# Loading w_q in ten transfers instead of two: eight of 16 rows and two of 64 rows

## The chip, the core and the metric

The kernel runs on one core of a Trainium2 chip, as one launch. The metric is the device time of the launch in microseconds, median of three runs. A profiled execution of the same kernel gives the trace; its span runs from the first to the last instruction, and the device time is a little longer than the span.

## The reference, cut to what matters

One decode step (one new token, batch 2) of a block that normalises x, runs attention over the last 4096 entries of a key and value cache with 32 query heads on 8 key heads, and multiplies the result by a gate from a small gated MLP:

```
xn = layernorm(x)                          # x: 2 x 1 x 512
q  = (xn @ wq) as 32 heads of 128          # wq: 512 x 4096
k, v = the last 4096 rows of each of 2 x 8 cache heads, 128 wide
o  = softmax(q k^T / sqrt(128)) v          # 4 query heads share a cache head
s  = o @ wo                                # wo: 4096 x 512
z  = gelu(xn @ w_in)                       # w_in: 512 x 1792
g  = w_sp * layernorm(z[896:]) + b_sp
y  = (z[:896] * g) @ w_out                 # w_out: 896 x 512
out = x + s * silu(y)
```

All of it is float32. What has to be read is 8 MB of w_q, 3.5 MB of w_in, 1.75 MB of w_out, 64 MB of keys and values, and 8 MB of w_o.

## The kernel before, in words

All large data goes through one ring of four SBUF slots (`ring`, `bufs=4`), each 128 partitions x 8192 float32, so 32 KB a partition and 4 MB in all. The tiles in the order in which they take a slot are wq0, wq1 (the two halves of w_q), win, wout, then k0, k1, v0, k2, v1, ... for eight units of attention (a unit is two cache heads), and last the pieces of w_o. All of these loads are issued on the SP queue, in the order of the code; a load that reuses a slot waits until the engines have finished with what was there.

w_q is viewed as 128 partitions x 4 rows x 4096 (`wq_v`, L93): partition p holds rows 4p to 4p+3 of w_q, 64 KB in a piece in memory. The first half, wq0, is the first two of these four rows (32 KB in a piece), the second half, wq1, the other two. The loop at L95 to L98 loads each half with one transfer of 128 rows of 32 KB.

After the loads the code makes small constants on POOL and DVE, normalises x and turns it (xnT). Then PE forms q: the loop over k at L202 runs 32 matmuls on wq0 (k = 0, 1) and 32 on wq1 (k = 2, 3) into the PSUM banks q_ps. The first needs all of wq0, the 33rd all of wq1. Then comes the MLP (z from win, y from wout), then the eight attention units: DVE turns a key tile in four parts (kt), PE makes the scores (sh, s), ACT the exponentials (p), and PE weighs the values (acc). The last part multiplies by w_o, whose last pieces are small (8, 8, 8, 4, 2, 1 and 1 of its 32 row blocks), and writes the 4 KB result.

Three tiny loads are issued on ACT's queue at the start: xs (x itself, 4 KB) and the two scalars of wb1 (4 bytes each).

How a load reports that it has landed matters to the change. The program gives each load one of eight completion counters in turn (DMAHW0 to DMAHW7 in the listings below). A load that takes a counter again first waits, on the queue that issues it, until the load that had the counter before has landed.

Of the kernel before, what the change touches and what calls it, by code (L numbers as in the profile page):

```python
# [14 lines left out]
P = 128  # L15
# [27 lines left out]
def kernel(  # L43
# [14 lines left out]
    pe, dve, act, sp = (InOrder(tc, e) for e in (nc.tensor, nc.vector, nc.scalar, nc.sync))  # L58
# [22 lines left out]
    def slot(name):  # L81
        return ring.tile([P, SLOT], F32, tag="slot", name=name)
# [10 lines left out]
    wq_v = wq.rearrange("(p k) f -> p k f", p=P)  # L93
    wqt = []
    for a in range(2):  # L95
        t = slot(f"wq{a}")
        sp.dma_start(t, wq_v[:, 2 * a : 2 * a + 2, :].rearrange("p k f -> p (k f)"))
        wqt.append(t.rearrange("p (k f) -> p k f", k=2))  # L98
    win = slot("win")[:, : KT * F]
    sp.dma_start(win, w_in.rearrange("(p k) f -> p (k f)", p=P))  # L100
# [325 lines left out]
    for i, piece in enumerate(pieces):  # L426
        t = slot(f"wo{i}").rearrange("p (j d) -> p j d", d=D)
# [54 lines left out]
    for n in range(EARLY):  # L482
        t, a = blocks[n]
# [5 lines left out]
    for n in range(EARLY, 32):  # L489
        if n == LATE:  # L490
            spread_quarters(so, parts, start=False, stop=False)
        t, a = blocks[n]
# [37 lines left out]
```

## Time and profile before

| | |
|---|---|
| device time, median of 3 runs | 217.5 us (217.49 to 217.58) |
| profiled execution: device time | 217.5 us |
| profiled execution: span | 215.7 us, so 1.8 us lie outside it |
| busy: PE, DVE, ACT | 155.7, 108.5, 44.1 us |
| load queue of SP (q1) | 89.40 MB in 3912 packets, 96.8% of 16 engines' span |
| mean rate | 415 GB/s |

The page divides the span into 40 slices of 5.4 us and gives, for each, the busy share of every engine in tenths, the share for which the 16 DMA engines were busy, and the GB/s that they moved. The tables by stretch give the same for freely chosen stretches, with a DMA share that can come out a little over or under 1, since a packet is counted in the stretch in which it starts. A packet of q1 is one row of a tile, or a small message of a few bytes that reports that an engine has finished its part of a transfer.

### The profile page before, as it was taken

What the parts mean: (1) busy time and instruction counts of PE and PEld (TensorE: products, weight loads), DVE (VectorE), ACT (ScalarE), POOL (GpSimd) and SP (SyncE); (2) the same over time, 40 slices, a digit from 0 to 9 for tenths busy, and PEclk for the clock granted to TensorE, in tenths of its full rate; (3) what the DMA queues carried; (4) which work ended last, traced back from release to release, by engine and by line L of the source; (5) the groups of instructions that cost most, each with busy time, mean ns of one, the idle gap of its engine ahead of it and who ended that gap; (6) DMA issues with size and microseconds to landing.
All of it is one profiled execution on the core that took longest, in us unless ns stands there. A gap on an engine that the chain in (4) does not pass through costs nothing.

```text
span 215.7 us, 2229 instructions
## 1 busy us (share of the span) xinstructions
PE 155.7 (72%) x866; PEld 43.6 (20%) x866; DVE 108.5 (50%) x176; ACT 44.1 (20%) x109; POOL 2.6 (1%) x14
## 2 busy tenths in 40 slices
PE   0164856151796997899699599459959948998883
PEld 0110212110121222222122222222212212231311
DVE  3400072425976944963946851685577089240101
ACT  5000001401123115114303404120431421242001
POOL 4000000000000000000000000000000000000000
PEclk9999788755589699799889879958988995999699
DMA  7998999999999999999999999999999999999990
GB/s 292 389 486 389 425 433 454 451 416 431 444 395 474 395 459 413 450 425 431 437 400 456 413 444 428 431 437 431 431 407 453 419 444 431 431 401 416 425 377 35
DMA packets 3929, 89.54 MB, mean 415 GB/s; under 512 B 446, under 2 KB 462, under 8 KB 848
## 3 DMA queue, kind: packets, MB, share of 16 engines
q1 hardware_dynamic: 3912, 89.40, 96.8%
q8 instruction: 7, 0.11, 0.2%
q14 instruction: 2, 0.02, 0.0%
q10 hardware_dynamic: 8, 0.00, 0.0%
HBM read 89.40 MB, written 0.00 MB: 414 GB/s over the span
## 4 chain that ended last, share of the span: by engine, by line
DMA 44%; PE 31%; DVE 19%; issue 3%; ACT 1%; SPq 0%; DVEq 0%
DMA k<-in_A_k_cache_dram 22%; DMA win<-in_B_w_in_dram 14%; DVE kt L37 13%; PE s L37 9%; PE sh L37 9%; DMA wo<-in_A_wo_dram 8%; PE acc L37 6%; PE z L37 2%; PE y L37 2%; PE mo L37 1%; DVE gate L37 1%; PE col L37 1%; PE so L37 1%; DVE u L37 1%; DVE m L37 1%
## 5 line engine op out<-in xcount | busy, mean ns | idle before, releaser
L37 DVE STREAM_TRANSPOSE kt<-k 128x2048 f32<-128x2048 f32 x32 | 72.4, 2293 | 24.9 <-DMA k<-in_A_k_cache_dram 24.9
L37 PE MATMUL sh<-kt,qbd 128*32 128x512 f32 x256 | 41.5, 682 | 14.0 <-DVE kt L37 14.0
L37 PE MATMUL s<-shs,add_dq 128*128 128x512 f32 x64 | 41.0, 748 | 0.0
L37 ACT ACTIVATE shs<-sh 128x512 f32<-128x512 f32 x32 | 19.1, 597 | 100.9 <-PE sh L37 100.9
L37 PE MATMUL acc<-v,pT 128*32 128x512 f32 x256 | 32.0, 641 | 0.2 <-DVE pT L37 0.2
L37 PE MATMUL q_ps<-wq,xnT 128*32 128x512 f32 x64 | 11.0, 850 | 9.9 <-DMA wq<-in_A_wq_dram 9.9
L37 PEld LDWEIGHTS s<-shs,add_dq 128*128 128x128 f32 x64 | 11.2, 219 | 28.3 <-issue 23.9
L37 PEld LDWEIGHTS sh<-kt,qbd 128*32 128x32 f32 x256 | 6.9, 115 | 33.9 <-issue 19.6
L37 PEld LDWEIGHTS acc<-v,pT 128*32 128x32 f32 x256 | 7.7, 118 | 25.8 <-issue 23.0
L37 DVE TENSOR_REDUCE m<-s 128x2 f32<-128x512 f32 x8 | 5.4, 680 | 14.0 <-PE s L37 14.0
L37 PE MATMUL mo<-l,same_r 128*128 128x2 f32 x16 | 3.5, 287 | 10.7 <-ACT p L37 10.7
L37 DVE STREAM_TRANSPOSE qT<-q_ps 128x512 f32<-128x512 f32 x2 | 1.4, 717 | 18.1 <-PE q_ps L37 18.1
L37 ACT ACTIVATE o<-acc,wd 128x128 f32<-128x128 f32 x32 | 9.1, 373 | 3.4 <-PE acc L37 3.4
L37 ACT ACTIVATE p<-s,nb 128x256 f32<-128x256 f32 x16 | 7.6, 490 | 7.1 <-DVE nb L37 6.9
L37 PE MATMUL part<-wo,oT 128*32 128x512 f32 x56 | 8.2, 722 | 1.1 <-DMA wo<-in_A_wo_dram 0.8
L37 PE MATMUL col<-o,sel 128*32 128x512 f32 x16 | 8.3, 601 | 0.4 <-ACT o L37 0.4
L37 ACT ACTIVATE zs<-z 128x448 f32<-128x448 f32 x1 | 0.5, 544 | 30.9 <-PE z L37 30.9
L37 PE MATMUL y<-wout,hT 128*32 128x512 f32 x14 | 3.6, 1059 | 3.8 <-issue 3.8
L37 PEld LDWEIGHTS q_ps<-wq,xnT 128*32 128x32 f32 x64 | 2.6, 144 | 17.1 <-issue 12.2
L37 DVE STREAM_TRANSPOSE pT<-p 128x512 f32<-128x512 f32 x8 | 5.4, 675 | 1.2 <-ACT p L37 1.2
L37 DVE TENSOR_TENSOR res<-so,gate 128x128 f32<-128x128 f32 x1 | 0.3, 292 | 11.1 <-PE so L37 11.1
L37 ACT ACT_TABLE_LOAD x4 | 5.1, 1283 | 1.9 <-issue 1.9
(106 smaller groups left out, 66.8 us busy)
## 6 DMA issues: line engine op xcount, KB each, us to landing
k<-in_A_k_cache_dram SPq DMA_DIRECT2D x8, 4096.0 KB, 21.3
v<-in_A_v_cache_dram SPq DMA_DIRECT2D x8, 4096.0 KB, 26.7
wq<-in_A_wq_dram SPq DMA_DIRECT2D x2, 4096.0 KB, 21.3
wo<-in_A_wo_dram SPq DMA_DIRECT2D x3, 2048.0 KB
win<-in_B_w_in_dram SPq DMA_DIRECT2D x1, 3584.0 KB, 29.3
wout<-in_B_w_out_dram SPq DMA_DIRECT2D x1, 1792.0 KB, 33.1
wo<-in_A_wo_dram SPq DMA_DIRECT2D x1, 1024.0 KB
wo<-in_A_wo_dram SPq DMA_DIRECT2D x1, 512.0 KB, 17.4
```

Of the source, the lines that this page charges most:

```text
L37: return self.tc.keep_in_program_order(call(*args, **kwargs))
```

## The change: what it does

The loop that loads the two halves of w_q issues several transfers for each half. The first half goes in eight transfers of 16 rows: transfer r takes partitions r, r+8, r+16, ..., r+120. The second half goes in two transfers of 64 rows: the even partitions, then the odd ones. Every row is still 32 KB in a piece, lands at the same place, and is loaded once.

```diff
     for a in range(2):
         t = slot(f"wq{a}")
-        sp.dma_start(t, wq_v[:, 2 * a : 2 * a + 2, :].rearrange("p k f -> p (k f)"))
+        rows = 16 if a == 0 else 64
+        for r in range(P // rows):
+            sp.dma_start(
+                t[r : P : P // rows, :],
+                wq_v[r : P : P // rows, 2 * a : 2 * a + 2, :].rearrange("p k f -> p (k f)"),
+            )
         wqt.append(t.rearrange("p (k f) -> p k f", k=2))
```

On the SP queue, at the start of the program, there stood before (wq_69 is the tile of the first half, wq_71 that of the second; in brackets what a load waits for, where `PE` and `DVE` mean the last reader of the slot):

```order
L37 DMA wq_69<-in_A_wq_dram 128x8192
L37 DMA wq_71<-in_A_wq_dram 128x8192
L37 DMA win<-in_B_w_in_dram 128x7168
L37 DMA wout<-in_B_w_out_dram 128x3584
L37 DMA k_281<-in_A_k_cache_dram 128x1x8192 [waits DMAHW1_49,PE_49]
L37 DMA k_283<-in_A_k_cache_dram 128x1x8192 [waits DMAHW4_49,DMAHW0_49,PE_49]
```

and now (wq_69 and wq_78 are the two halves):

```order
L37 DMA wq_69<-in_A_wq_dram 16x8192 x5
L37 DMA wq_69<-in_A_wq_dram 16x8192 [waits DMAHW0_49]
L37 DMA wq_69<-in_A_wq_dram 16x8192 [waits DMAHW1_49]
L37 DMA wq_69<-in_A_wq_dram 16x8192 [waits DMAHW2_49]
L37 DMA wq_78<-in_A_wq_dram 64x8192 [waits DMAHW3_49]
L37 DMA wq_78<-in_A_wq_dram 64x8192 [waits DMAHW4_49]
L37 DMA win<-in_B_w_in_dram 128x7168 [waits DMAHW5_49]
L37 DMA wout<-in_B_w_out_dram 128x3584 [waits DMAHW6_49]
L37 DMA k_289<-in_A_k_cache_dram 128x1x8192 [waits DMAHW2_49,DMAHW1_49,DMAHW7_49,DMAHW0_49,PE_49]
L37 DMA k_291<-in_A_k_cache_dram 128x1x8192 [waits DMAHW4_49,DMAHW3_49,PE_49]
```

Eight loads are added, and the first four loads of before, which waited for nothing, now stand behind waits on counters that are used a second time: DMAHW0 had xs, DMAHW1 the first piece of w_q, DMAHW2 and DMAHW3 the two scalars of wb1, DMAHW4 to DMAHW7 the second to fifth piece.

On PE, at the start of the q matmuls, there stood before:

```order
L37 MATMUL q_ps_149<-wq_69,xnT 32x512 [waits DMAHW1_49,DVE_49]
L37 MATMUL q_ps_149<-wq_69,xnT 32x512 x3
L37 MATMUL q_ps_150<-wq_69,xnT 32x512 x4
L37 MATMUL q_ps_149<-wq_69,xnT 32x512 x4
L37 MATMUL q_ps_150<-wq_69,xnT 32x512 x4
L37 MATMUL q_ps_149<-wq_71,xnT 32x512 [waits DMAHW4_49]
```

and now:

```order
L37 MATMUL q_ps_157<-wq_69,xnT 32x512 [waits DMAHW4_49,DMAHW5_49,DMAHW2_49,DMAHW6_49,DMAHW1_49,DMAHW7_49,DMAHW0_49,DVE_49]
L37 MATMUL q_ps_157<-wq_69,xnT 32x512 x3
L37 MATMUL q_ps_158<-wq_69,xnT 32x512 x4
L37 MATMUL q_ps_157<-wq_69,xnT 32x512 x4
L37 MATMUL q_ps_158<-wq_69,xnT 32x512 x4
L37 MATMUL q_ps_157<-wq_78,xnT 32x512 [waits DMAHW4_49,DMAHW3_49]
```

The matmuls and their order are the same; the first waits for all eight pieces of the first half, the 33rd for both of the second.

## The prediction, made before the changed kernel was run

> **What bounds the kernel now.** I read the page's slices and queues first, then a table by stretch, then single microseconds of the load queue, then the queue of SP and the end of the chain.
>
> The page, slices and queue (busy tenths of the 16 DMA engines, GB/s; packets, MB, share):
>
> ```profile
> DMA  7998999999999999999999999999999999999990
> GB/s 292 389 486 389 425 433 454 451 416 431 444 395 474 395 459 413 450 425 431 437 400 456 413 444 428 431 437 431 431 407 453 419 444 431 431 401 416 425 377 35
> ...
> q1 hardware_dynamic: 3912, 89.40, 96.8%
> ```
>
> By stretch (last two columns: DMA share and GB/s):
>
> ```profile
> 0.00:2.00 2.00, 0.00 (x0) 0.00 (x0) 0.57 (x2) 0.14 (x1) 1.45 (x11) 1.00 0.51 150
> 2.00:4.00 2.00, 0.00 (x0) 0.00 (x0) 0.99 (x3) 1.91 (x3) 1.18 (x4) 1.00 0.93 377
> 4.00:12.00 8.00, 0.61 (x4) 0.55 (x4) 3.05 (x20) 0.92 (x2) 0.00 (x0) 1.00 0.91 393
> 12.00:20.00 8.00, 5.67 (x32) 1.39 (x32) 0.00 (x0) 0.00 (x0) 0.00 (x0) 1.00 1.06 459
> 20.00:30.00 10.00, 5.34 (x32) 1.22 (x32) 2.77 (x10) 0.00 (x0) 0.00 (x0) 0.83 0.97 419
> ...
> 60.00:110.00 50.00, 42.60 (x218) 11.46 (x220) 35.08 (x40) 12.31 (x32) 0.00 (x0) 0.88 1.01 432
> 110.00:160.00 50.00, 40.47 (x220) 12.02 (x212) 29.05 (x36) 12.75 (x35) 0.00 (x0) 0.90 1.00 431
> 160.00:200.00 40.00, 34.29 (x182) 8.83 (x182) 20.25 (x30) 9.57 (x27) 0.00 (x0) 0.87 0.99 425
> ```
>
> The loads bound the kernel. From 2 us to the end of the last load the 16 engines are never idle, and they move 432 GB/s in a long stretch, 27.0 GB/s each; 89.40 MB at 432 GB/s is 206.9 us of a 215.7 us span. PE, DVE and ACT have room in every stretch. The chain of waits names other work too, but its last link of that kind is a load:
>
> ```profile
> 193.29 17.36 DMA wo<-in_A_wo_dram
> ...
> 210.70 1.24 PE so L37 x32
> ...
> 212.79 0.29 DVE res L37
> ```
>
> SP does wait for engines to free slots, yet it issues early enough that the share stays at 0.97 to 1.06. So a microsecond that the load engines lose at the start has nothing to be absorbed in, and moves the last w_o piece (210.66 us) and the end by a microsecond. PE work on w_q is no cover: it waits for the loads.
>
> One round of rows, from 7 to 8 us:
>
> ```profile
> DMA packets 17, 0.52 MB, mean 524 GB/s; under 512 B 1, under 2 KB 1, under 8 KB 1
> ...
> q1 hardware_dynamic: 16, 0.52, 121.3%
> q10 hardware_dynamic: 1, 0.00, 0.1%
> ```
>
> Sixteen rows of 32 KB start together: the engines go in step, one row each. 0.524 MB at 432 GB/s is 1.214 us a round, and a half of w_q is eight rounds, 9.71 us.
>
> **The change, part by part.**
>
> SP and its waits:
>
> ```profile
> 0.73 0.86 SPq L37 DMA_DIRECT2D wq<-in_A_wq_dram  x2
> 1.63 0.46 SPq L37 DMA_DIRECT2D win<-in_B_w_in_dram  x1
> 2.14 0.53 SPq L37 DMA_DIRECT2D wout<-in_B_w_out_dram  x1
> 18.63 9.83 SPq L37 DMA_DIRECT2D k<-in_A_k_cache_dram  x2
> ...
> 12.90 5.67 PE L37 MATMUL q_ps<-wq,xnT 128*32 128x512 f32 x32 [5.93 <-DMA wq<-in_A_wq_dram]
> 22.51 5.34 PE L37 MATMUL q_ps<-wq,xnT 128*32 128x512 f32 x32 [3.94 <-DMA wq<-in_A_wq_dram]
> ```
>
> *Issuing.* Eight more loads at 0.43 us (two took 0.86) are 3.4 us of SP. A piece feeds the engines for a 1.21 us round, so issuing stays ahead of moving: nothing. What is queued behind on SP is win and wout, then k0, which waits for PE until 18.63 us anyway.
>
> *Counters.* The sixth to eighth piece and wq1's first transfer wait for xs, the first piece and the two wb1 scalars; wq1's second, win and wout wait for pieces two to four, which land earlier. The scalars come last. Their queue is q10, eight packets in all; from 9 to 10 us, and from 10 to 12 us:
>
> ```profile
> q1 hardware_dynamic: 15, 0.49, 113.7%
> q10 hardware_dynamic: 1, 0.00, 0.1%
> ...
> q1 hardware_dynamic: 17, 0.56, 64.4%
> ```
>
> The last q10 packet starts before 10 us. Then wq1 can be issued, while the eight pieces keep the engines fed to about 12 us (4.20 MB have started by then by the first three stretches, one half of w_q). From first issue to the flow was 0.9 to 1.5 us (0.73 to about 2.28, where 4.20 MB at 432 GB/s would have begun). So the margin is 12.0 - 10.0 - 1.5 = 0.5 us at the least: nothing. If rounds take twice as long, so do the q10 packets, one to a round, and so does the supply; the margin grows. If that cover fails, see the rivals.
>
> *Reports of completion.* Eight more transfers put eight more small packets on each engine. q1 is busy 0.968 x 215.7 = 208.8 us and its bytes need 206.9; if all of the 1.9 us were the reports of 27 transfers, that is 0.07 us each and 0.56 us for eight. The other end is 0, since the 7-to-8 us row shows a small packet beside 16 full rows. I take 0.1, nearer to that row.
>
> *Where the rows land.* This decides. Before, a round of 16 rows can be dealt from all 128 partitions. Now each round of the first half is one transfer: 16 rows, at partitions r, r+8, ..., r+120, with seven of eight partitions untouched, for r = 0 to 3 one set of groups of four and for r = 4 to 7 the other. The steady 27.0 GB/s an engine, alike for weights and caches and for rows of 32 and 16 KB, looks like a fixed cap. If it is the engine's own, the stride costs 0. If it is a cap of paths into the tile, each serving some partitions, two engines share a path and a round takes 2 x 1.214 us: eight rounds cost 9.71 us more. No transfer in this trace with large rows leaves partitions out, so no row lies near either end; a gain is excluded from a rate that is already at the cap in all stretches. I take the shared path: a limit at memory would hardly be equal for such different sources, and half the groups of partitions idle in each round is the pattern in which a limit by partition must show. Two engines that aren't quite in step share a path a little less; for this I take off 0.3 us (0 to 1.2, one round).
>
> [...]
>
> *The second half.* Rows at stride 2 touch every group of four partitions. Each transfer has four rows for an engine, all groups in use: I take 0; the other end is 9.71, if engines in step aim at the same groups at the same time. The nearest row is that of 60 to 110 us: the cache loads have 64 x 2 rows as their source, and ran at 432.
>
> Sum: 217.5 (the profiled execution, equal to the median) + 9.7 - 0.3 + 0.1 = 227.0 us. Landings: wq0 12.9 to 22.4, wq1 22.5 to 32, win 31 to 40.5, all later ones 9.5 later. What is late next is nothing new: k0's issue waits for PE on wq0 (18.6 to 28), and wq1, win and wout keep the engines fed past 45 us.
>
> **The rivals.**
>
> *Engines don't share (no change).* Only reports remain: 217.5 + 0.1 = 217.6, from 217.3 to 218.1. For it: 27.0 GB/s may be the engine's own. Against: the argument above. 22%.
>
> *Both halves share.* 217.5 + 9.4 + 9.7 + 0.1 = 236.7. For it: engines in step. Against: the cache loads. 15%.
>
> *The counters starve the queue.* It decides from the point where the second wb1 scalar lands later than about 11 us. If ACT's packets only get through when SP's eight pieces are done (12 us), wq1 comes 0.9 to 1.5 us after, so 219.0 without sharing. Against: one q10 packet starts in each microsecond from 7 to 10. 6%.
>
> *The pieces don't go one row to an engine.* If partitions fix the engine, pieces 0 to 3 use eight engines with two rows each and 4 to 7 the others, which begin four issues (1.7 us) later: 219.3. The trace can't tell, all transfers having 128 rows. 5%. [...]
>
> *Faster.* A first transfer of one row each might start all engines sooner. 4.20 MB by 12.0 us leave 2.28 - 0.73 = 1.55 us from issue to flow; half of that saved gives 216.8. The only cover-free gain I see; nothing shows the start to depend on the size of the transfer. 4%.
>
> **How the numbers follow.** Sharing in the first half alone has 45%, with 226.0 to 228.0 as its own range; some sharing of smaller size (218 to 226) 3%. Taking in the cases from no change to the first half gives 217.2 to 228.0, with 15% (both halves) and 4% (faster) outside. 0.2% is 0.4 us, about what a measurement of this kernel can tell. Faster 5%: that rival, and a little of the case without sharing. Same 18%: most of the 22%. Slower 77%: the rest.
>
> **What would show it.** First PE matmul on wq0 at about 22.4 us, on wq1 at 32; in the stretch from 4 to 20 us some 216 GB/s, and 432 again from 24 us on. If wq0 lands at 13 us, the stride costs nothing and the forecast is wrong at its main step. If 216 GB/s lasts to 40 us, both halves share. If the DMA share drops below 0.9 with rows of the old length, it is the counters.

## The result, and the profile after

The changed kernel took 228.1 us (median of five runs, 228.0 to 228.75) against 217.54 us before: 10.6 us longer, a ratio of 1.0491, 95% interval 1.0476 to 1.0506. Forecast were 227.0 us and a range of 217.2 to 228.0; the way was right, the time lies 0.1 us above the range.

The page of the changed kernel, slices of 5.66 us and load queue:

```profile
DMA  8999899999999999999999999999999999999991
GB/s 186 185 220 237 376 440 405 446 423 459 408 423 457 411 428 454 411 428 452 417 428 439 423 434 440 420 434 434 417 440 440 414 440 434 423 411 428 420 390 42
...
q1 hardware_dynamic: 4040, 89.40, 96.9%
```

The load engines are as busy as before, but the first four slices move about half as much: 185 to 237 GB/s. The bytes are the same, and the 128 packets more are the reports of eight transfers on 16 engines. The table by stretch (last columns: DMA share and GB/s) shows where it ends:

```profile
0.00:2.00 2.00, 0.00 (x0) 0.00 (x0) 0.57 (x2) 0.03 (x1) 1.45 (x11) 1.00 0.01 2
2.00:22.50 20.50, 0.61 (x4) 0.55 (x4) 4.05 (x24) 2.94 (x4) 1.19 (x4) 1.00 1.03 221
...
24.00:34.00 10.00, 6.42 (x36) 1.57 (x37) 0.00 (x0) 0.00 (x0) 0.00 (x0) 0.89 1.00 429
34.00:200.00 166.00, 129.27 (x658) 35.15 (x654) 99.96 (x139) 37.14 (x92) 0.00 (x0) 0.82 1.00 431
```

From 24 us on the rate is 429 to 431 GB/s, that of the kernel before. So the second half, in two transfers of 64 rows at stride 2, loads at full rate; nearly all that is lost is lost on the first half. One round of it, from 6.6 to 9.15 us:

```profile
DMA packets 32, 0.52 MB, mean 206 GB/s; under 512 B 16, under 2 KB 16, under 8 KB 16
...
q1 hardware_dynamic: 32, 0.52, 100.6%
```

Sixteen rows and their sixteen reports in 2.55 us, where a round of before took 1.21. Sixteen rows keep the sixteen engines busy for that time (share 100.6%): one row to an engine, and each engine needs 2.1 times as long for it.

The trace has the start and the duration of every packet, and the rows of w_q give the whole loss round by round. The rows of the first round start 0.26 us later on average than in the kernel before, and take 0.58 us longer (2.25 for 1.67). Those of six rounds take 1.33 us longer (2.55 for 1.21), those of the fifth round, the first with r = 4 to 7, 1.18 us (2.39 for 1.21), and those of the first round of the second half 0.51 us (1.72 for 1.21). Together that is 10.5 us; from the next round on, the rows are 10.6 us later than before.

SP and PE in the changed kernel:

```profile
0.73 8.27 SPq L37 DMA_DIRECT2D wq<-in_A_wq_dram  x10
...
23.86 5.83 PE L37 MATMUL q_ps<-wq,xnT 128*32 128x512 f32 x32 [16.84 <-DMA wq<-in_A_wq_dram]
33.27 6.24 PE L37 MATMUL q_ps<-wq,xnT 128*32 128x512 f32 x32 [3.58 <-DMA wq<-in_A_wq_dram]
42.69 4.53 PE L37 MATMUL z<-win,xnT 128*32 128x448 f32 x32
```

PE starts on the first half at 23.86 us instead of 12.90, on the second at 33.27 instead of 22.51, 11.0 and 10.8 later. At the end, the chain's last link is a load as before, and PE begins its last work 10.7 us later than in the kernel before (210.70 there):

```profile
204.30 17.09 DMA wo<-in_A_wo_dram
221.38 0.04 issue
221.43 1.68 PE so L37 x40
```

Nothing absorbed the loss and nothing added to it on the way.

### The profile page after: what moved, and what is told of

Read it like the earlier page. It is cut to its first block, busy times and chain, and to the rows that moved or that the text cites. A ratio compares the mean times of both kernels' runs of the same rounds, so it can differ in the third digit from the quotient of the medians.

```text
span 226.4 us, 2241 instructions
## 1 busy us (share of the span) xinstructions
PE 157.0 (69%) x866; PEld 44.0 (19%) x866; DVE 108.5 (48%) x176; ACT 44.0 (19%) x109; POOL 2.6 (1%) x14
## 4 chain that ended last, share of the span: by engine, by line
DMA 42%; PE 33%; DVE 19%; issue 3%; ACT 1%; SPq 0%; DVEq 0%
DMA k<-in_A_k_cache_dram 21%; DMA wq<-in_A_wq_dram 14%; DVE kt L37 13%; PE s L37 9%; PE sh L37 8%; DMA wo<-in_A_wo_dram 8%; PE acc L37 5%; PE q_ps L37 3%; PE z L37 2%; PE y L37 2%; PE mo L37 1%; DVE gate L37 1%; PE col L37 1%; PE so L37 1%; DVE u L37 1%
## 5 line engine op out<-in xcount | busy, mean ns | idle before, releaser
L37 PE MATMUL s<-shs,add_dq 128*128 128x512 f32 x64 | 41.5, 755 | 0.0
L37 ACT ACTIVATE shs<-sh 128x512 f32<-128x512 f32 x32 | 19.1, 597 | 100.6 <-PE sh L37 100.6
L37 PE MATMUL q_ps<-wq,xnT 128*32 128x512 f32 x64 | 12.1, 926 | 20.4 <-DMA wq<-in_A_wq_dram 20.4
L37 PE MATMUL mo<-l,same_r 128*128 128x2 f32 x16 | 3.5, 287 | 10.6 <-ACT p L37 10.6
L37 PEld LDWEIGHTS q_ps<-wq,xnT 128*32 128x32 f32 x64 | 3.1, 164 | 28.6 <-issue 28.6
L37 DVE TENSOR_TENSOR res<-so,gate 128x128 f32<-128x128 f32 x1 | 0.3, 292 | 10.7 <-PE so L37 10.7
```

The source lines that it names most:

```text
L37: return self.tc.keep_in_program_order(call(*args, **kwargs))
```

## The experiments

My theory was that of the prediction: the cap is one of paths into the tile, each serving some partitions, and a transfer is as fast as the paths that it reaches allow. No trace shows such a path, how many there are or which partitions share one. I count here by groups of four neighbouring partitions, as in the prediction. All 128 rows, 64 rows at stride 2 and 32 rows at stride 4 touch every group of four, and were to load at the 432 GB/s of the kernel before. 16 rows at stride 8 and 64 neighbouring rows touch half of the groups, and were to load at half of that, two engines to a path. 16 neighbouring rows touch an eighth of them; the four engines to a path that I expected there don't follow from this count, and no run shows them. What is called a shared round below is a slow one: sixteen rows in 2.55 us in the changed kernel, where the kernel before took 1.21. The rivals were the number or the size of the transfers, the distances at which memory is read, and the start of the queue. All experiments change only the loop that loads w_q; the other half is loaded whole, in one transfer of 128 rows, unless said. Of each edit only the lines that matter are shown.

### Which half, and which property of a transfer

**Second half alone** (`e1_half2_only`):

```diff
+        sets = [slice(0, P)] if a == 0 else [slice(r, P, 2) for r in range(2)]
+        for s in sets:
+            sp.dma_start(t[s, :], wq_v[s, 2 * a : 2 * a + 2, :].rearrange("p k f -> p (k f)"))
```

> First half whole (128 rows), second half in two transfers of 64 rows at stride 2. Sharing of paths by groups of partitions: stride 2 touches every group, so no cost: 217.5 to 217.8 us, rows of 1.21 us. Rival, that several small transfers cost by themselves: two instead of one, 218 or more.

Measured: 217.61 us, ratio 1.0005 (0.9996 to 1.0015). No cost can be told.

**First half alone** (`e2_half1_only`): `sets = [slice(r, P, 8) for r in range(8)] if a == 0 else [slice(0, P)]`

> First half in eight transfers of 16 rows at stride 8, second half whole. Sharing: all of the loss of the changed kernel, 227.9 to 228.2 us, rows of 2.55 us in the first half only. Rival, that both halves add to it: 0.3 us or more below the changed kernel's 228.1.

Measured: 228.09 us, ratio 1.0490 (1.0474 to 1.0506): the whole loss.

**First half in two blocks of 64 neighbouring rows** (`e3_two_blocks_of_64`): `sets = [slice(64 * r, 64 * r + 64) for r in range(2)] if a == 0 else [slice(0, P)]`

> First half in two transfers of 64 neighbouring rows (0 to 63, 64 to 127), second half whole. Sharing: each transfer reaches half of the groups, as the 16 rows did, so rows of 2.5 us and 227.5 to 228.5 us although the transfers are as large as in the cheap second half of the changed kernel. Rival, that the smallness of the transfers (512 KB, one row to an engine) costs: 217.5 to 218.

Measured: 228.56 us, ratio 1.0506 (1.0491 to 1.0522). One round, from 6.6 to 9.17 us (no report of q1 in it; the one small packet is of q10):

```profile
DMA packets 17, 0.52 MB, mean 204 GB/s; under 512 B 1, under 2 KB 1, under 8 KB 1
...
q1 hardware_dynamic: 16, 0.52, 99.6%
q10 hardware_dynamic: 1, 0.00, 0.0%
```

This is the experiment that decides between size and partitions. Its two transfers are as many and as large as the two of the cheap second half; only the partitions are neighbours instead of every second one. It costs as much as eight transfers of 16 rows. The two also stand in different halves of w_q; the next run puts a stride into the first half.

**First half in four transfers of 32 rows at stride 4** (`e4_four_of_32_step4`): `sets = [slice(r, P, 4) for r in range(4)] if a == 0 else [slice(0, P)]`

> First half in four transfers of 32 rows at stride 4, second half whole. Each transfer has one row in each group of four partitions. Sharing, with the rows dealt so that an engine stays in its groups: no cost, 217.5 to 218. Sharing, with neighbouring rows of a transfer dealt to one engine: engines in step meet at the same groups, about 228. Rival, that smallness costs: between, some 220 to 224.

Measured: 218.17 us, ratio 1.0030 (1.0018 to 1.0042). Its rate from 5 to 21 us is 426 GB/s:

```profile
5.00:21.00 16.00, 5.62 (x36) 1.88 (x36) 3.03 (x20) 0.00 (x0) 0.00 (x0) 1.00 0.99 426
```

So one row in each group of four neighbouring partitions gives nearly the rate of the kernel before, 436 GB/s in the same stretch. The 0.64 us that remain are a little more than I had expected (218 at most), and are looked at below.

**First half in eight blocks of 16 neighbouring rows** (`e5_eight_blocks_of_16`): `sets = [slice(16 * r, 16 * r + 16) for r in range(8)] if a == 0 else [slice(0, P)]`

> [...] Sharing: four engines on a path, rows of 4 x 1.21 to 4 x 1.27 = 4.9 to 5.1 us, eight rounds some 39 to 41 us, 246 to 249 us in all. Rival (number or size of transfers): 228.

Measured: 243.14 us (one run), 25.7 us above the kernel before on that chip. One round, from 9.35 to 13.72 us, takes 4.4 us:

```profile
DMA packets 34, 0.52 MB, mean 120 GB/s; under 512 B 18, under 2 KB 18, under 8 KB 18
...
q1 hardware_dynamic: 32, 0.52, 100.5%
```

As many transfers of the same size as in the changed kernel, and 15 us slower than it: which partitions a transfer writes decides, and the order is the one expected, 206 GB/s with half of the groups of four and 120 with an eighth. The size of the step was missed: 3.6 times an unshared round, not 4 to 4.2. That four engines meet on a path there is shown by no run. One thing was overlooked: each block of 16 writes other groups of four than the block before it, so every round follows a switch of groups, and the run on the order of the transfers, below, shows shorter rounds with such switches (2.33 us for 2.55). Whether that explains the 3.6 was not tested.

### The reading side

**Source rows close together** (`e6_source_close`):

```diff
+                sp.dma_start(t[r:P:8, :], wq_v[16 * r : 16 * r + 16, 0:2, :].rearrange("p k f -> p (k f)"))
```

> As the half with eight transfers of 16 rows at stride 8, but from 16 neighbouring rows of w_q instead of every eighth (the rows so land on other partitions than the reference needs); second half whole. Engines then read 64 KB apart instead of 512 KB. Sharing on the way into the tile: 228, as before; if the 5% by which a shared row is slower than twice an unshared one come from the reading side, rows of 2.43 and 227.2. Rival (reading at large distances is what costs): 217.6.

Measured: 228.56 us, ratio 1.0510 (1.0493 to 1.0528), and a round from 6.65 to 9.2 us as slow as before:

```profile
DMA packets 32, 0.52 MB, mean 206 GB/s; under 512 B 16, under 2 KB 16, under 8 KB 16
```

Not the distance between the rows that are read, then, and the 5% above twice the time don't come from there either.

**Source rows far apart** (`e7_source_far`): the whole tile in one transfer, `ap=[[4 * SLOT, P], [1, SLOT]]` on the key cache.

> First half as one transfer of 128 rows, but read from the key cache at a distance of 128 KB from row to row, so the values of q are not the reference's; second half whole. Sharing on the way into the tile: no cost, 217.5 to 217.8. Rival (reading at large distances costs): 222 or more.

Measured: 217.42 us (one run; 217.45 for the kernel before on that chip, whose runs in all the experiments lie between 217.33 and 217.95). Reading far apart costs nothing, and reading close together saved nothing: the loss hangs on the partitions that are written.

### Engines in step

**The eight transfers in the order 0, 4, 1, 5, 2, 6, 3, 7** (`e8_alternate`): `sets = [slice(r, P, 8) for r in (0, 4, 1, 5, 2, 6, 3, 7)] if a == 0 else [slice(0, P)]`

> First half in eight transfers of 16 rows at stride 8, taken in the order 0, 4, 1, 5, 2, 6, 3, 7, second half whole. Each next transfer is on the other set of groups. In the changed kernel the one round after such a switch took 2.39 us instead of 2.55, since the engine that is ahead leaves the path to the other. Sharing with this effect: six more switches save 6 x 0.15 = 0.9 us, about 227.1. If the switch has no such effect: 228.

Measured: 226.91 us (226.72 to 227.21), ratio 1.0434 (1.0419 to 1.0450), 1.2 us below the order 0 to 7 (228.09, ratio 1.0490, for the first half alone). A round, from 8.53 to 10.86 us:

```profile
DMA packets 32, 0.52 MB, mean 225 GB/s; under 512 B 16, under 2 KB 16, under 8 KB 16
```

2.33 us instead of 2.55. Only the order of equal transfers changed, so 1.2 us of the loss hang on which transfer follows which. My explanation, that the engine ahead leaves the path free, predicted the sign and most of the size (0.9 of 1.2 us); what the engines do inside a round was not seen directly, so it stays an argument.

### The start

SP's first issue in the kernel before (start, duration):

```profile
0.73 0.39 SPq L37 DMA_DIRECT2D wq<-in_A_wq_dram  x1
```

and in the changed one:

```profile
0.73 0.63 SPq L37 DMA_DIRECT2D wq<-in_A_wq_dram  x1
```

It took 0.59 us in the kernel with four of 32, and 0.41 in that with blocks of 16. In the runs that begin with strided rows (0.59 to 0.63), or with 64 neighbouring rows (0.57), the first issue is about 0.2 us longer, and in the first 2 us next to nothing moves (2 GB/s, where the kernel before has 150). In the changed kernel the first row starts at 2.14 us instead of 1.75. The longer issue is 0.24 us of these 0.39; the rest isn't explained.

**The other half first, then four of 32 at stride 4** (`e9_covered_issue`):

```diff
+    halves = [slot(f"wq{a}") for a in range(2)]
+    for a in (1, 0):
+        sets = [slice(r, P, 4) for r in range(4)] if a == 0 else [slice(0, P)]
+        for s in sets:
+            sp.dma_start(halves[a][s, :], wq_v[s, 2 * a : 2 * a + 2, :].rearrange("p k f -> p (k f)"))
```

> The second half, whole, is issued first; then the first half in four transfers of 32 rows at stride 4. With the first half in front, that form took 218.17 us, and its rows began to move 0.35 us later than those of the kernel before, after an issue of about 0.59 us instead of 0.40. Theory, that the longer first issue and the start are its whole cost: covered by the other half it is nothing, 217.4 to 217.7. Rival, that four transfers cost by themselves wherever they stand: 218.1.

Measured: 217.80 us, ratio 1.0025 (1.0012 to 1.0038), just above what the theory gave. The median gives back 0.37 us of the 0.64, but the intervals of the two kernels (1.0018 to 1.0042 for the other) overlap widely. In the first 2 us its loads move as in the kernel before:

```profile
0.00:2.00 2.00, 0.00 (x0) 0.00 (x0) 0.57 (x2) 0.13 (x1) 1.45 (x11) 1.00 0.58 166
```

The traces say more than the medians. With four of 32 in front, the rows of w_q's second round are 0.51 us later than in the kernel before, and those of the later rounds 0.53 to 0.55. With the other half in front, no round behind the first is more than 0.05 us late. The last link of the chain that is a load says the same. In the kernel before, PE could go on from it at 210.66 us. With four of 32 in front, with the other half in front, and in the control that follows, in this order:

```profile
193.07 18.04 DMA wo<-in_A_wo_dram
192.83 17.96 DMA wo<-in_A_wo_dram
194.10 16.67 DMA wo<-in_A_wo_dram
```

These end at 211.11, 210.80 and 210.78 us. So what this form costs the loads, 0.45 us, arises at the start, and is gone when the other half covers it. The 0.3 us by which the covered form is still above the kernel before lie behind the loads: its last DVE instruction starts at 212.87 us and that of the control at 212.88, and the spans are 216.1 and 215.8 us. Each of these is one profiled execution.

**Both halves whole, the second first** (`e10_swapped_whole`): as above with `sets = [slice(0, P)]`.

> Both halves whole, the second issued first: the control of the two others of this set. No change, 217.4 to 217.7.

Measured: 217.57 us, ratio 1.0007 (0.9998 to 1.0015): the swap itself is nothing.

**The other half first, then eight of 16 at stride 8** (`e11_covered_sharing`): as above with `sets = [slice(r, P, 8) for r in range(8)]` for the first half.

> The second half, whole, is issued first; then the first half in eight transfers of 16 rows at stride 8. Sharing alone, without the start: eight rounds of 2.55 us instead of 1.21, less 0.15 at the change of the set of groups, and a slower round before or after: 10.5 to 11 us, 228.0 to 228.5. If the start made a part of the loss: 227.6 or less.

Measured: 228.16 us, ratio 1.0487 (1.0473 to 1.0500): the same loss without the late start. Sharing alone can make all of it. The first shared round costs 0.79 us here (2.01 for 1.21). In front it costs 0.58, and the later start 0.26; why the first shared round is cheaper in front isn't shown.

## Why the prediction was right or wrong, point by point

- **The bound** was right. The loads bound the kernel: 10.8 us lost at the first matmul on the second half of w_q are 10.7 us at the last w_o pieces and 10.6 in the device time.
- **Where the rows land**, the deciding step, was right in kind: about half the rate, in the first half alone, with the writing side as the cause. The experiments with 64 neighbouring rows, with 16 neighbouring rows and with the two sources show it, and they rule out size, number and reading. No run shows the paths themselves, how many there are or which partitions have one in common. So two engines to a path, from which the 9.7 us of the sum come, is shown by no run; what the runs showed in its place is 2.55 us a round (206 GB/s) instead of 1.21 for 16 rows at stride 8, which touch half of the groups of four, and 426 GB/s for 32 rows at stride 4, with one row in each.
- **The term that was mis-sized is this one.** I had a shared round at exactly twice an unshared one, 2.43 us, and took off 0.3 us for engines out of step, for which no row stood. A shared round takes 2.55 us, and the only relief is in the one round behind the switch from r = 3 to r = 4 (2.39). Sharing cost the rows of w_q 10.3 us, against the 9.4 of the sum, and the later start another 0.26. So of the 1.1 us between 227.0 and 228.1, 0.6 are dearer rounds, 0.3 are the amount taken off, and the rest is about the size of the later start. The range failed with it: I had let sharing be cheaper than half the rate, but not dearer, though no row stood for either end. Why a shared round takes 5% more than twice an unshared one is open: it isn't the distance of the reads (206 GB/s with the source rows close together too).
- **Issuing at nothing** was wrong in its place. The later issues are covered, as I had it, although one takes 0.59 us (the median of the ten) and not 0.43. The first one is not covered, and it is 0.24 us longer (0.63 for 0.39). This hardly shows in the total of the changed kernel, as the run with the half loaded second shows.
- **The counters** cost nothing, as forecast. The last four of q10's eight packets start between 4 and 7 us, earlier than I had said and not one to a round (the line below). What comes last is not the scalars, as I had it, but pieces two to four of the slow first half: wq1's second transfer, win and wout wait for them, and are issued at 8.5, 11.1 and 13.5 us. That is early enough, since the rows of the first half keep the engines busy past 22 us; the share of 1.03 up to 22.5 us leaves no gap.

```profile
q10 hardware_dynamic: 4, 0.00, 0.1%
```

- **Reports of completion**: 16 of them are in a round with 16 rows, beside 2.55 us; the round of 64 neighbouring rows without them is no shorter (2.57). So next to nothing, as taken.
- **The second half** at nothing: right (1.0005).
- **The rivals.** No sharing: out. Both halves: out (second half alone, 1.0005). Starved queue: out (share 1.03). Rows not one to an engine: out, since 16 rows keep all 16 engines busy for a round (100.6%). Faster by a smaller first transfer: no. With a smaller first transfer the first row starts at 2.07 to 2.14 us instead of 1.75, but for the blocks of 16, where it starts at 1.76.

## What to carry to other kernels

When the load engines are the bound, look at which partitions each transfer writes. Here 64 rows at stride 2 cost nothing (1.0005), and 32 at stride 4 cost 0.64 us, 0.45 of it by their late start; both touch every group of four. 64 neighbouring rows or 16 at stride 8 left a little less than half the rate (204 and 206 of 432 GB/s), 16 neighbouring rows little over a quarter (120). Look for it in the GB/s at a DMA share of 1: in this case a full share with half the rate (100.6% at 206 GB/s) was engines that needed 2.1 times as long for a row, and not a queue without work. And when a rate is taken to be shared, let the range include that sharing itself costs something: here a round took 2.55 us, more than twice 1.21.

## What the runs showed that I had not expected

- Half of the groups of four gave less than half of the rate: 206 GB/s with 16 rows at stride 8 and 204 with 64 neighbouring rows, where half of 432 is 216. A round in the order 0, 4, 1, 5 moved 225 GB/s, and one in the blocks of 16 moved 120, where an eighth of 432 is 54; in both, each transfer writes other groups than the one before. What sets these rates stays open.
- The order of equal transfers was worth 1.2 us (228.09 to 226.91): a shared round was shorter where the next transfer writes the other groups of four (2.33 us) than where it writes the same (2.55).
- The first issue on SP took 0.39 us for 128 rows or 0.41 for 16 neighbouring ones, but 0.57 to 0.63 with a stride or 64 rows.
